# A recurrence, an MLP and a top-1 MoE on one core: other places for small products, routers, low parts, gathers and the end branch

## Chip, cores and metric

One core of one Trainium2 chip runs the whole kernel. The metric is the device time of one execution in microseconds. Engines are called as in the profile: PE (matmuls), PEld (weight loads), DVE, ACT, POOL, and SP, which issues most transfers.

## What is computed

Three stages follow one another; the output of each is the input of the next.

```
for t in range(768):                     # B=4, H=8, D=40
    y[:, :, t] = einsum('bhd,bhde->bhe', r_t, state)
    Sa = einsum('bhde,bhe->bhd', state, a_t)
    state = state * w_t[:, :, None, :] - einsum('bhd,bhe->bhde', Sa, b_t) + einsum('bhd,bhe->bhde', v_t, k_t)
x = y as [3072 tokens, 320]
x = relu(x @ w_in) ** 2 @ w_out          # 320 -> 2048 -> 320
e = argmax(x @ w_gate)                   # 8 experts, capacity 768 each
out = softmax(x @ w_gate)[e] * (relu(x @ w1[e]) @ w2[e])
```

## The kernel before

**Stages.** The sequence is cut into 12 segments of 64 tokens, and each segment into two chunks `c` of 32. The recurrence is solved chunk by chunk: per segment a lower-triangular system is inverted step by step on POOL (`rw.invert`, lines 333, with transposes to and from its layout on DVE at L220 and L242), and per chunk some hundreds of small products on PE (L336) carry the state. Their tiles are named `pr` (right side, `rw.right`), `psa` and `psd` (solve and turn), `ppq` (inner and mix), `pn` (state step, added into `zv` by DVE at L350), `py` (output, multiplied into `y` by DVE at L435 and L436) and `pa` (the next but one segment's matrix, `rw.lower`, read by `rw.put`, L201). `rw.scale` makes the scaled keys and decays of a segment by scans on DVE (L127, L140).

The MLP of a segment (256 columns for the 4 batch entries) is eight *bursts*: `up` makes two feature tiles `pl` of 16 matmuls (L494), in two pieces of 8, ACT forms the square `g` and its rounded copy `gh`, DVE the low part `gl` = g - gh (L705); `down` adds 12 matmuls into `acc` (L678) in two pieces, of which 4 read `gl`. A burst goes down after two later ones have gone up (`BEHIND = 2`). Before the segments there are 17 *routers* of two pieces each (`routers`): each folds one tile of `w_out` with `w_gate` (`ptg`, L501; `pog`, L678; `wogl`, L457), from `ao` tiles that DVE splits at L564 to L575.

The MoE handles 15 units of 256 tokens in its usual run, more behind a branch. Per unit: POOL gathers the unit's rows (`gather`, L1195, into the two buffers of `xg`), `turn` transposes them and makes the gate (L1216), four pairs of up (`upl`, L494) and down (`uacc`, L1187) follow, `end` multiplies by the gate (`uo`, DVE L1254 for the first 128 rows, ACT L1255 for the second), and two scatters on POOL write the result (L1265). Before the first unit the places of the first units are worked out by `early` (`ea_rank`, `solve_op` at L1009, `ea_inv`).

**What sets the order.** PE keeps program order for all these matmuls (`keep_in_program_order`); the other engines' orders come from a scheduler that follows priority, which is program order with offsets. The program is a loop over `s` and `c`; each chunk is a list of slots (`slot_a` to `slot_g`: output and right side; solve; burst; turn and inner; steps; mix; state step, and in chunk 1 the inverse, `lower` twice and `put`). After each slot `mlp(n)` issues `n` pieces of the MLP (or routers), where `n` comes from the tables `FIRST` (s = 0), `SECOND` (s = 1) and `SLOTS` (later):

```
for part, n in zip(parts, (FIRST, SECOND, SLOTS)[min(s, 2)][c]):
    with ahead(s):
        part()
    next(sc, None)
    mlp(n)
    ...
    next(side or iter(()), None)
```

`side` is the generator of `early`, which goes one step per slot. At the end `others` loads the number of units (L1307) and branches to further units; behind it L1598 loads `good`, a flag that the decays were in range, and L1599 branches to a slow path if not.

Of the kernel before, what the change touches and what calls it, by code (L numbers as in the profile page):

```python
# [11 lines left out]
F32 = mybir.dt.float32  # L12
# [504 lines left out]
class Mlp:  # L517
# [132 lines left out]
    def load_gate(self):  # L650
        self.turn = self.routed = self.done = 0
        self.wo = {}
        self.slow = self.behind = None
        self.pending = []
# [36 lines left out]
    def up(self, s, x, fp):  # L691
        nc, NT = self.nc, self.NT
        pl = self.psl.tile([128, 2, NT], F32, tag="pl", name=f"pl{s}_{fp}")
        for f in range(2):
            ft = fp * 2 + f
            product(self.tc, pl[:, f], self.wi, slice(ft * 128, (ft + 1) * 128), x, slice(0, NT))
            if f == 0:
                yield
        g = self.tile([128, 2, NT], f"g{s}_{fp}", "relu", 2)
        nc.scalar.activation(g, pl, AF.Relu)  # L700

        gh = self.tile([128, 2, NT], f"gh{s}_{fp}", "gh", 2, F32R)
        gl = self.tile([128, 2, NT], f"gl{s}_{fp}", "gl", 2, F32R)
        nc.scalar.activation(g, g, AF.Square)
        self.behind = (nc.scalar.copy(gh, g).ins, nc.vector.tensor_tensor(out=gl, in0=g, in1=gh.bitcast(F32), op=ALU.subtract).ins)  # L705
        self.pending.append([self.down, s, fp, gh, gl, None])
        yield

# [35 lines left out]
    def drain(self, n):  # L744

        while len(self.pending) > n:
            self.lows()
            f, *a = self.pending.pop(0)
            yield from f(*a)
# [92 lines left out]
class Moe:  # L842
# [6 lines left out]
    def __init__(self, keep, tc, ps, ml, ident, x1, logits, w1, w2, cap, cst, out):  # L849
        self.tc, self.nc, self.ps, self.ml, self.ident = tc, tc.nc, ps, ml, ident  # L850
        self.x1, self.logits, self.w1, self.w2, self.out = x1, logits, w1, w2, out
        nc = self.nc
        ct = keep.tile([128, cst.shape[1]], F32, tag="w_d", name="ct2")
        nc.scalar.dma_start(out=ct, in_=cst)
        self.c = {k: ct[:, v] for k, (n, v) in SETS.items() if n == 1}
        self.room = keep.tile([128, 2 * 16 * SC], F32, tag="kb_d", name="room")
        self.at, self.free = {}, 0
        self.new("ue", [128, NU * NEXP])
        cpi = self.new("cpi", [128, 1], I32)
        nc.scalar.dma_start(out=cpi, in_=cap.bitcast(I32)[0, 0:1].partition_broadcast(128))  # L860
# [5 lines left out]
        self.ui, self.idx, self.gate = {}, {}, {}  # L866
# [100 lines left out]
    def experts(self, end, name, j0, j1):  # L967
# [14 lines left out]
        self.total = ui[0:1, n:n + 1]  # L982

# [216 lines left out]

    def turn(self, j, xs):
# [35 lines left out]
    def down(self, j, w2, h, fp):  # L1237
        if fp == 0:
            self.acc = [self.ml.psa.tile([128, DX], F32, tag=f"acc{t}", name=f"uacc{j}_{t}")[:, 0:DM] for t in range(2)]
        for f in range(2):  # L1240
            ft = fp * 2 + f
            for t in range(2):
                cols = slice(t * 128, (t + 1) * 128)
                for n, (a, b) in enumerate(((h[0], w2[0]), (h[0], w2[1]), (h[1], w2[0]))):
                    self.mm(self.acc[t], lhsT=a[:, f, cols], rhs=b[:, ft],
                            start=ft == 0 and n == 0, stop=ft == FE // 128 - 1 and n == 2)
# [22 lines left out]
    def unit(self, j, units):  # L1269
# [7 lines left out]
        for fp in range(FE // 256):  # L1277
            if fp == 0 and more:
                nxt = self.gather(j + 1)
# [7 lines left out]
            if fp == TURN_AT and more:  # L1287
                self.ready[j + 1] = self.turn(j + 1, nxt)
# [16 lines left out]
    def others(self):  # L1305

        n = self.nc.values_load(self.total, min_val=0, max_val=NU)  # L1307
# [52 lines left out]
USUAL = 15  # L1360
BEHIND = 2
# [5 lines left out]
SLOTS = (2, 3, 2, 3, 2, 3, 3), (4, 3, 2, 2, 3)  # L1367
LEAD = 4
SECOND = (2, 2, 2, 1, 2, 1, 3), (3, 1, 2, 1, 2)
FIRST = (8, 4, 4, 4, 4, 2, 2), (2, 2, 2, 2, 0)  # L1370
# [14 lines left out]
def in_range(tc, pool, ps, consts, rng):  # L1385
# [5 lines left out]
    n = pool.tile([1, 1], I32, name="good")  # L1391
    p = ps.tile([128, 512], F32, tag="ps", name="pgood")
    tc.nc.tensor.matmul(p[0:1, 0:1], lhsT=f, rhs=consts["lane"], start=True, stop=True)
    V.tensor_copy(n, p[0:1, 0:1])
    return n
# [3 lines left out]
def tile_rwkv__mlp__moe(ctx, tc, wd, kb, ad, rv, wl, tok, vt, nat, w_in, w_out, w_gate, w1, w2, cap, cst1, cst2, cst3, out):  # L1399
# [9 lines left out]
    with ExitStack() as ph:  # L1409
# [56 lines left out]
        for s in range(NS):  # L1466
# [3 lines left out]
            for c in range(NC):  # L1470
# [7 lines left out]
                def slot_a():  # L1478
# [8 lines left out]
                    if last is not None:  # L1487
                        y = rw.out(*last)
                    rw.right(s, c)

                def slot_b():
# [18 lines left out]
                    if c == 1:  # L1510
                        next(st, None)
                        if s + 2 < NS:
                            rw.place(s + 2, 1)
                    elif s + 2 < NS:
# [36 lines left out]
                parts = slot_a, slot_b, slot_c, slot_d, slot_e, slot_f, slot_g  # L1551
                if c == 1:
                    parts = slot_a, slot_b, slot_d, slot_f, slot_g
# [21 lines left out]
        good = in_range(tc, cp, ps, consts, rng)  # L1575
# [112 lines left out]
```

## Time and profile before

| | us |
|---|---|
| three runs | 1059.51, 1054.82, 1055.98 |
| median | 1055.98 |
| profiled execution (the first of these) | 1059.51 |
| its span, first to last instruction | 1057.7 |
| PE, DVE, ACT, POOL busy | 883.6, 753.5, 617.0, 536.0 |
| mean granted clock of PE | 0.962 |

PE is busy for 84% of the span. The stages lie one after another in the trace: up to 172 us weights, routers and the first two chunks; from 172 to 694 us the recurrence with the MLP in its gaps, one segment per 53 us; to 785 us the last segment's MLP; to 1038 us the MoE; then the tail.

### The profile page before, as it was taken

How to read it: one execution, taken by the hardware profiler on the slowest of the kernel's cores; microseconds unless marked ns; L12 is line 12 of the kernel's file. 1: busy time of each engine (PE TensorE's matmuls, PEld its weight loads, DVE VectorE, ACT ScalarE, POOL GpSimd, SP SyncE). 2: the span in 40 equal slices, each digit the busy share in tenths (PEclk: the TensorE clock that was granted, in tenths of full speed). 3: DMA queues.
4: the chain of work that ended last, by engine and by line, in shares of the span. 5: the costliest groups of instructions: out<-in, count | busy, mean ns of one | idle time of the engine just before them, and what ended most of it. 6: DMA issues, size and time to landing. Idle time of an engine off the chain costs nothing.

```text
span 1057.7 us, 38842 instructions
## 1 busy us (share of the span) xinstructions
PE 883.6 (84%) x15962; PEld 833.8 (79%) x15962; DVE 753.5 (71%) x1691; ACT 617.0 (58%) x1618; POOL 536.0 (51%) x863
## 2 busy tenths in 40 slices
PE   1048555989898999899989989999899979999992
PEld 1047445888887998898888888999799979989992
DVE  7879778476768586768676766555579858778760
ACT  2135444765665666667656657765484757677650
POOL 4878508577686758686868685600000322223210
PEclk9999996999998999899999999999899999999996
DMA  7673464675565656565656564552682767777710
GB/s 210 194 235 94 142 177 115 222 207 168 143 189 139 180 151 180 148 180 165 175 145 180 148 169 135 150 154 67 223 267 80 237 177 222 226 203 228 212 54 9
DMA packets 91212, 177.17 MB, mean 168 GB/s; under 512 B 16489, under 2 KB 46827, under 8 KB 90060
## 3 DMA queue, kind: packets, MB, share of 16 engines
q1 hardware_dynamic: 87196, 164.99, 54.6%
q0 software_dynamic: 2880, 8.98, 2.5%
q8 instruction: 129, 2.11, 0.9%
q10 hardware_dynamic: 944, 0.57, 0.2%
q14 instruction: 63, 0.52, 0.2%
HBM read 138.52 MB, written 16.24 MB: 146 GB/s over the span
## 4 chain that ended last, share of the span: by engine, by line
PE 49%; DMA 15%; DVE 12%; ACT 9%; issue 7%; POOL 4%; SPq 2%; ACTq 0%; POOLq 0%; DVEq 0%
PE pl L494 12%; PE acc L678 11%; PE upl L494 7%; PE uacc L1187 7%; DMA out_dram<-uo,room 3%; DMA rq_a<-in_ad_dram 3%; PE pn L336 2%; POOL tl L333 2%; DVE zv L350 2%; DMA kb_d<-in_kb_dram 2%; PE ppq L336 2%; PE psa L336 2%; POOL tmp L333 2%; DVE rq_r L127 1%; DMA stage_lo<-in_w_out_dram 1%
## 5 line engine op out<-in xcount | busy, mean ns | idle before, releaser
L333 POOL TENSOR_TENSOR tl<-tl,tmp 128x126 f32<-128x126 f32 (+22 forms) x372 | 239.0, 642 | 29.0
L333 POOL TENSOR_TENSOR tmp<-solve_al,tl 128x126 f32<-128x126 f32 (+22 forms) x372 | 200.2, 538 | 61.2 <-DVE solve_al L220 28.6
L705 DVE TENSOR_TENSOR gl<-g,gh 128x512 fp32r<-128x512 f32 x96 | 66.7, 695 | 97.7 <-ACT gh L705 97.1
L678 PE MATMUL acc<-woh,gh 128*128 128x328 f32 x384 | 126.6, 335 | 4.0 <-ACT x L730 4.0
L678 PE MATMUL acc<-wol,gh 128*128 128x328 f32 x384 | 120.0, 318 | 0.8 <-issue 0.8
L494 PE MATMUL pl<-x_hi,wi_hi 128*128 128x256 f32 x384 | 118.2, 308 | 0.5 <-ACT x_hi L506 0.5
L494 PE MATMUL pl<-x_lo,wi_hi 128*128 128x256 f32 x384 | 112.4, 293 | 5.1 <-DVE x_lo L509 5.1
L494 PE MATMUL pl<-x_hi,wi_lo 128*128 128x256 f32 x384 | 112.1, 292 | 1.1 <-issue 1.1
L1265 POOL DMA_INDIRECT out_dram<-uo,room x30 | 34.3, 1142 | 152.4 <-DVE uo L1254 82.3
L1195 POOL DMA_INDIRECT xg<-x_dram,room x30 | 29.9, 997 | 145.4 <-DVE room L1027 69.6
L700 ACT ACTIVATE g<-pl 128x512 f32<-128x512 f32 x96 | 57.3, 597 | 68.4 <-PE pl L494 67.3
L678 PE MATMUL acc<-woh,gl 128*128 128x328 f32 x384 | 90.6, 318 | 0.0
L1187 PE MATMUL uacc<-w2h,hh 128*128 128x320 f32 x240 | 76.3, 318 | 11.9 <-DVE uo L1254 11.9
L494 PEld LDWEIGHTS pl<-x_lo,wi_hi 128*128 128x128 f32 x384 | 76.7, 200 | 5.4 <-DVE x_lo L509 5.4
L494 PEld LDWEIGHTS pl<-x_hi,wi_hi 128*128 128x128 f32 x384 | 76.4, 199 | 5.2 <-issue 1.2
L678 PEld LDWEIGHTS acc<-woh,gh 128*128 128x128 f32 x384 | 74.2, 193 | 7.2 <-ACT x L730 4.3
L494 PEld LDWEIGHTS pl<-x_hi,wi_lo 128*128 128x128 f32 x384 | 76.5, 199 | 0.0
L1187 PE MATMUL uacc<-w2h,hl 128*128 128x320 f32 x240 | 75.1, 313 | 0.0
L1187 PE MATMUL uacc<-w2l,hh 128*128 128x320 f32 x240 | 75.0, 312 | 0.0
L678 PEld LDWEIGHTS acc<-wol,gh 128*128 128x128 f32 x384 | 74.3, 194 | 0.0
L336 PE MATMUL pa<-kb_d,rq_a 40*32 40x64 f32 x1536 | 29.5, 236 | 52.8 <-DVE rq_a L167 47.2
L336 PEld LDWEIGHTS pa<-kb_d,rq_a 40*32 40x32 f32 x1536 | 26.5, 119 | 54.6 <-DVE rq_a L167 47.4
(264 smaller groups left out, 2710.3 us busy)
## 6 DMA issues: line engine op xcount, KB each, us to landing
wol<-wol SPq DMA_DIRECT2D x96, 328.0 KB
w<-in_w_dram SPq DMA_DIRECT2D x30, 640.0 KB
w<-in_w_dram SPq DMA_DIRECT2D x30, 512.0 KB
zv<-in_vt_dram SPq DMA_DIRECT2D x48, 208.0 KB
kb_d<-in_kb_dram SPq DMA_DIRECT2D x24, 320.0 KB
tk<-in_tok_dram SPq DMA_DIRECT2D x24, 320.0 KB
rx<-rt SPq DMA_DIRECT2D x192, 40.0 KB
zk<-tk SPq DMA_DIRECT2D x48, 160.0 KB
```

What stands on the lines that cost most here:

```text
L127: nc.vector.tensor_tensor_scan(out=rf[:, ::-1], data0=w[:rows, 1:][:, ::-1], data1=seed, initial=0.0, op0=ALU.mult, op1=ALU.add)
L333: self.last = f(*a, **k).ins
L336: self.tc.keep_in_program_order(self.nc.tensor.matmul(*a, **k))
L350: i = nc.vector.tensor_tensor(out=each(z[c ^ 1][rows, j, ps]), in0=each(z[c][rows, j, ps]), in1=pn[rows].rearrange("p (n y) e -> p n y e", ...
L494: tc.keep_in_program_order(tc.nc.tensor.matmul(out, lhsT=a, rhs=b, start=n == 0, stop=n == len(seq) - 1))
L678: self.tc.keep_in_program_order(self.nc.tensor.matmul(*a, **k))
L700: nc.scalar.activation(g, pl, AF.Relu)
L705: self.behind = (nc.scalar.copy(gh, g).ins, nc.vector.tensor_tensor(out=gl, in0=g, in1=gh.bitcast(F32), op=ALU.subtract).ins)
L1187: self.tc.keep_in_program_order(self.nc.tensor.matmul(*a, **k))
L1195: nc.gpsimd.indirect_dma_start(out=xg[:, 0:DX], out_offset=None, in_=self.x1, in_offset=bass.IndirectOffsetOnAxis(ap=self.idx[2 * j + t], ...
L1265: self.nc.gpsimd.indirect_dma_start(out=self.out, out_offset=bass.IndirectOffsetOnAxis(ap=self.to[:, n:n + 1], axis=0), in_=o[:, t], in_of ...
```

## The change

Seven edits, each small in code.

- **Slots.** `slot_r` takes `right` out of `slot_a`; chunk 1's `slot_g` is cut into `slot_g` (state step), `slot_h` (inverse, first `lower`, `put`) and `slot_i` (second `lower`, `put`). The tables have an entry for each; a chunk issues 18 and 14 pieces as before in `SLOTS`.
- **Routers.** `FIRST` gives 16 pieces (eight routers) after the first slot, none after the right side, and fewer between the solve and the mix.
- **Third scale.** `rw.scale(2)` is made in chunk 1 of segment 0 instead of chunk 0, and `place(2, 1)` in its last slot.
- **Low parts.** `gl` is issued after the first half of the next `up` (`low_parts`), no longer with `gh`.
- **Gathers.** `gather(j + 2)` is asked for right after `turn(j + 1)`, at the third of unit j's pairs, no longer at the start of unit j + 1; unit 1's with unit 0's turn.
- **Last pair of a unit.** The down products of the last pair go tile by tile: the six of the first accumulator, then the six of the second.
- **End branch.** `bad` (64 if out of range, else 0) is added to the number of units; one load serves both branches.

```diff
+                self.low_parts()
...
-        self.behind = (nc.scalar.copy(gh, g).ins, nc.vector.tensor_tensor(out=gl, in0=g, in1=gh.bitcast(F32), op=ALU.subtract).ins)
-        self.pending.append([self.down, s, fp, gh, gl, None])
+        self.behind = nc.scalar.copy(gh, g).ins, self.behind[1] if self.behind else None
+        self.pending.append([self.down, s, fp, gh, g, None])
+        self.whole.append(self.pending[-1])
...
+    def low_parts(self):
+        while self.whole:
+            p = self.whole.pop(0)
+            s, fp, gh, g = p[1:5]
+            p[4] = self.tile([128, 2, self.NT], f"gl{s}_{fp}", "gl", 2, F32R)
+            i = self.nc.vector.tensor_tensor(out=p[4], in0=g, in1=gh.bitcast(F32), op=ALU.subtract)
+            self.behind = self.behind[0], i.ins
...
+    def ask(self, j, units):
+        if j in units and j not in self.asked and 2 * j in self.idx:
+            self.asked[j] = self.gather(j)
...
+        order = [(f, t) for f in range(2) for t in range(2)]
+        if fp == FE // 256 - 1:
+            order = [(f, t) for t in range(2) for f in range(2)]
...
-                self.ready[j + 1] = self.turn(j + 1, nxt)
+                self.ready[j + 1] = self.turn(j + 1, self.asked.pop(j + 1))
+                self.ask(j + 2, units)
...
-SLOTS = (2, 3, 2, 3, 2, 3, 3), (4, 3, 2, 2, 3)
+SLOTS = (2, 2, 3, 2, 2, 2, 3, 2), (2, 2, 3, 2, 2, 1, 1, 1)
-SECOND = (2, 2, 2, 1, 2, 1, 3), (3, 1, 2, 1, 2)
-FIRST = (8, 4, 4, 4, 4, 2, 2), (2, 2, 2, 2, 0)
+SECOND = (0, 2, 2, 2, 1, 2, 1, 3), (1, 2, 1, 2, 1, 1, 1, 0)
+FIRST = (16, 0, 2, 2, 2, 2, 2, 2), (0, 2, 2, 2, 0, 0, 0, 0)
...
-                        if s + 2 < NS:
+                        if 0 < s < NS - 2:
                             rw.place(s + 2, 1)
-                    elif s + 2 < NS:
+                    if s + 2 < NS and c == (s == 0):
                         sc = rw.scale(s + 2)
...
-                    if c == 1 and more:
+                def slot_h():
+                    if more:
                         rw.inverted(s + 1)
                         if s + 2 < NS:
                             rw.lower(s + 2, 0)
                             rw.put()
-                            rw.lower(s + 2, 1)
-                            rw.put(True)
...
-        mo.others()
-    n = nc.values_load(good[0:1, 0:1], min_val=0, max_val=128)
-    with tc.If(n != 128):
+        n = nc.values_load(mo.state[0:1, 0:1], min_val=0, max_val=NU + BAD)
+        rest = ph.enter_context(tc.If(n > USUAL))
+        mo.others(n)
+        ph.close()
+    with tc.If(n >= BAD):
```

**Order on PE, steady segment, end of chunk 1** (state step `pn`, matrices `pa`, then the up products `pl` or down products `acc` of a burst; x32 means 32 rows alike). Before, both state steps and both matrices follow one another:

```order
L678 MATMUL acc_1_4429<-woh,gl_3_4533 128x328
L336 MATMUL pn_1_0_4818<-zv_117,zk_122 40x40 x16
L336 MATMUL pn_1_1_4837<-zv_117,zk_122 40x40 x16
L336 MATMUL pa_0_4862<-kb_d,rq_a_4163 32x64 x32
L336 MATMUL pa_1_4902<-kb_d,rq_a_4163 32x64 x32
L494 MATMUL pl_6_4938<-x_hi,wi_hi 128x256
```

Of the change:

```order
L336 MATMUL pn_1_0_4802<-zv_117,zk_122 40x40 x16
L336 MATMUL pn_1_1_4821<-zv_117,zk_122 40x40 x16
L678 MATMUL acc_0_4426<-woh,gh_3_4532 128x328
L678 MATMUL acc_0_4426<-wol_3_4535,gh_3_4532 128x328
L678 MATMUL acc_1_4427<-woh,gh_3_4532 128x328
L678 MATMUL acc_1_4427<-wol_3_4535,gh_3_4532 128x328
L678 MATMUL acc_0_4426<-woh,gl_3_4633 128x328
L678 MATMUL acc_1_4427<-woh,gl_3_4633 128x328
L336 MATMUL pa_0_4854<-kb_d,rq_a_4161 32x64 x32
```

Six down products now stand between the state step and the first matrix; six more follow it, and then the second matrix.

**Order on PE in the startup**, before (the first right side `pr` ahead of the routers, `psa` behind four of them):

```order
L336 MATMUL pa_1_833<-kb_d,rq_a_778 32x64 x32
L336 MATMUL pr_0_938<-zv_116,a_114 32x40 x32
L501 MATMUL ptg<-ct,ao_160 128x128 x2
L501 MATMUL ptg<-ct,ao_160 64x128
L501 MATMUL ptg<-ct,ao_171 128x128 x2
```

and of the change, the same place and the end of the routers:

```order
L501 MATMUL ptg<-ct,ao_389 128x128 x2
L501 MATMUL ptg<-ct,ao_389 64x128
L678 MATMUL pog<-wg,wt_1016 128x8 x3
L336 MATMUL pr_0_1039<-zv_116,a_114 32x40 x32
L336 MATMUL psa_0_1074<-rh_0_1072,tt_789 32x40 x32
L501 MATMUL ptg<-ct,ao_400 128x128 x2
L501 MATMUL ptg<-ct,ao_400 64x128
L678 MATMUL pog<-wg,wt_1030 128x8 x3
```

Before, four routers stand between this `pr` and `psa`, and four between `psa` and `psd`; of the change, eight stand ahead of `pr`, none between it and `psa`, and two between `psa` and `psd`.

**Order on DVE, steady segment, end of chunk 1** (`gl` the low part, `y` the output, `zv` the state, `x_lo` the next MLP input). Before:

```order
L705 TENSOR_TENSOR gl_6_4958<-g_6_4955,gh_6_4957 128x512
L435 TENSOR_TENSOR y_1_5012<-py_1_4979,qt_1_3887 128x320
L436 TENSOR_TENSOR y_1_5012<-py_1_4979,qt_1_3887 128x64
L393 TENSOR_TENSOR zv_116<-zv_116,g_4_3075 40x8x2x40 x2
L509 TENSOR_TENSOR x_lo<-pt,x_hi 128x8x32
```

Of the change:

```order
L435 TENSOR_TENSOR y_1_4987<-py_1_4954,qt_1_3862 128x320
L436 TENSOR_TENSOR y_1_4987<-py_1_4954,qt_1_3862 128x64
L393 TENSOR_TENSOR zv_116<-zv_116,g_4_3073 40x8x2x40 x2
L716 TENSOR_TENSOR gl_6_5209<-g_6_5000,gh_6_5002 128x512
L509 TENSOR_TENSOR x_lo<-pt,x_hi 128x8x32
```

The low part now stands behind the output and the state's decay.

On POOL the gathers and scatters of the MoE stand in the same order in both kernels.

## Rows read from the trace of the kernel before

**Rows 1.** Busy time by stage: us; each engine's busy us (instructions); granted clock; DMA share; GB/s.

```profile
0.00:172.00 172.00, 69.27 (x1391) 59.41 (x1391) 142.57 (x303) 63.34 (x184) 101.93 (x169) 0.95 0.60 173
222.50:648.70 426.20, 396.68 (x9322) 370.35 (x9321) 309.77 (x528) 269.07 (x632) 308.97 (x516) 0.96 0.59 163
785.00:1038.00 253.00, 240.82 (x1824) 237.86 (x1822) 190.69 (x583) 164.26 (x509) 58.00 (x54) 0.99 0.61 177
```

**Rows 2.** Waits of PE from 172 to 785 us: waiter, releaser; total us, times, longest.

```profile
PE pr L336 <- issue: 6.7, 4, 3.0
PE pt L501 <- DVE y L436: 6.3, 5, 3.2
PE pr L336 <- DVE zv L350: 6.1, 12, 1.7
PE pa L336 <- issue: 5.1, 6, 1.5
PE pz L307 <- issue: 1.8, 1, 1.8
PE ea_inv L1187 <- DVE solve_op L1009: 2.4, 1, 2.4
```

**Rows 3.** Timeline of PE round 587 us: start, us, instruction, idle before it in brackets.

```profile
583.90 1.88 PE L336 MATMUL pa<-kb_d,rq_a 40*32 40x64 f32 x120
587.31 0.32 PE L336 MATMUL pa<-kb_d,rq_a 40*32 40x64 f32 x8 [1.53 <-issue]
```

**Rows 4.** DMA queues from 585 to 587.3 us: packets, MB, share.

```profile
q8 instruction: 1, 0.02, 3.0%
```

**Rows 5.** Two stretches by busy time and granted clock (columns of rows 1).

```profile
587.30:590.70 3.40, 3.39 (x22) 3.30 (x22) 3.30 (x7) 1.79 (x4) 0.87 (x3) 0.54 0.71 200
437.00:444.20 7.20, 7.20 (x95) 6.86 (x96) 4.58 (x8) 5.80 (x15) 6.50 (x10) 0.53 0.31 87
```

**Rows 6.** Timeline of DVE: the same transpose in two successive segments.

```profile
427.77 1.23 DVE L242 STREAM_TRANSPOSE solve_tf<-tl 128x1024 f32<-128x1024 f32 x1
480.95 1.23 DVE L242 STREAM_TRANSPOSE solve_tf<-tl 128x1024 f32<-128x1024 f32 x1
```

**Rows 7.** Waits of POOL from 222 to 650 us.

```profile
POOL tl L333 <- DVE solve_tf L242: 57.3, 8, 9.0
POOL tmp L333 <- DVE solve_al L220: 21.6, 8, 2.9
```

**Rows 8.** Waits of DVE from 172 to 750 us.

```profile
DVE gl L705 <- ACT gh L705: 93.1, 45, 5.6
```

**Rows 9.** Timeline of DVE and PE: a low part and its first reader.

```profile
527.07 0.69 DVE L705 TENSOR_TENSOR gl<-g,gh 128x512 fp32r<-128x512 f32 x1 [1.29 <-ACT gh L705]
534.57 0.47 PE L678 MATMUL acc<-woh,gl 128*128 128x328 f32 x2
```

**Rows 10.** Timeline of PE (two rows) and DVE (three) in the startup.

```profile
77.37 1.29 PE L336 MATMUL psa<-rh,tt 32*32 32x40 f32 x64 [12.83 <-DVE tt L246]
165.02 0.87 PE L501 MATMUL pt<-ct,y 128*128 128x128 f32 x3 [10.05 <-DVE y L436]
72.31 1.25 DVE L242 STREAM_TRANSPOSE solve_tf<-tl 128x1024 f32<-128x1024 f32 x1 [4.50 <-POOL tl L333]
74.25 2.33 DVE L127 TENSOR_TENSOR_SCAN rq_r<-w_d,seed_q 104x1040 f32<-104x1040 f32 x1
118.87 0.29 DVE L565 TENSOR_SCALAR a<-a 128x256 f32<-128x256 f32 x1 [3.46 <-ACT a L564]
```

**Rows 11.** The placing of the first units, by busy time (columns of rows 1).

```profile
730.30:748.80 18.50, 16.07 (x287) 13.23 (x286) 17.41 (x74) 6.29 (x15) 0.00 (x0) 0.98 0.14 39
```

**Rows 12.** Waits of PE from 785 to 1045 us.

```profile
PE uacc L1187 <- DVE uo L1254: 11.9, 5, 5.3
```

**Rows 13.** Lines 1598 and 1308 on POOL's sequencer: count, ns min/median/max, first and last start.

```profile
L1598 POOLq TENSOR_LOAD <-good x1: 304/304/304, 1046.9 to 1046.9; - x1
L1308 POOLq INC_SWDGE_SEM  x1: 1379/1379/1379, 1045.5 to 1045.5; - x1
```

More of the change, by code (lines that the diff above doesn't have):

```diff
@@ L653, in load_gate @@
         self.slow = self.behind = None
-        self.pending = []
+        self.pending, self.whole = [], []
         for k in range(3):
@@ L702, in up @@
         gh = self.tile([128, 2, NT], f"gh{s}_{fp}", "gh", 2, F32R)
-        gl = self.tile([128, 2, NT], f"gl{s}_{fp}", "gl", 2, F32R)
         nc.scalar.activation(g, g, AF.Square)
-        self.behind = (nc.scalar.copy(gh, g).ins, nc.vector.tensor_tensor(out=gl, in0=g, in1=gh.bitcast(F32), op=ALU.subtract).ins)
-        self.pending.append([self.down, s, fp, gh, gl, None])
+        self.behind = nc.scalar.copy(gh, g).ins, self.behind[1] if self.behind else None
+        self.pending.append([self.down, s, fp, gh, g, None])
+        self.whole.append(self.pending[-1])
         yield
+    def low_parts(self):
[5 more added lines that the diff above has]
+            self.behind = self.behind[0], i.ins
     def down(self, s, fp, gh, gl, wol):
@@ L747, in drain @@
             self.lows()
+            if self.pending[0] in self.whole:
+                self.low_parts()
             f, *a = self.pending.pop(0)
@@ L865, in __init__ @@
         self.ready, self.w1s, self.w2s, self.to, self.done = {}, {}, {}, None, []
-        self.ui, self.idx, self.gate = {}, {}, {}
+        self.bad = None
+        self.ui, self.idx, self.gate, self.asked = {}, {}, {}, {}
     def space(self, ctx):
@@ L982, in experts @@
         self.total = ui[0:1, n:n + 1]
+        if self.bad is not None:
+            both = self.new(f"{name}_both", [128, 1])
+            V.tensor_tensor(out=both[0:1], in0=uf[0:1, n:n + 1], in1=self.bad[0:1], op=ALU.add)
+            self.state = self.new(f"{name}_state", [128, 1], I32)
+            V.tensor_copy(self.state[0:1], both[0:1])
     def places(self, slot, name):
@@ L1084, in first @@
                 self.ready[0] = self.turn(0, self.xs)
+                self.ask(1, range(USUAL))
     def late(self, first):
@@ L1239, in down @@
             self.acc = [self.ml.psa.tile([128, DX], F32, tag=f"acc{t}", name=f"uacc{j}_{t}")[:, 0:DM] for t in range(2)]
[L1240 to L1246, printed above, removed]
+        order = [(f, t) for f in range(2) for t in range(2)]
+        if fp == FE // 256 - 1:
+            order = [(f, t) for t in range(2) for f in range(2)]
+        for f, t in order:
+            ft, cols = fp * 2 + f, slice(t * 128, (t + 1) * 128)
+            for n, (a, b) in enumerate(((h[0], w2[0]), (h[0], w2[1]), (h[1], w2[0]))):
+                self.mm(self.acc[t], lhsT=a[:, f, cols], rhs=b[:, ft],
+                        start=ft == 0 and n == 0, stop=ft == FE // 128 - 1 and n == 2)
         if fp == FE // 256 - 1:
@@ L1277, in unit @@
         for fp in range(FE // 256):
-            if fp == 0 and more:
-                nxt = self.gather(j + 1)
+            if fp == 0:
+                self.ask(j + 1, units)
             h = self.up(j, x, w, fp)
@@ L1303, in run, with others @@
             pass
-    def others(self):
-        n = self.nc.values_load(self.total, min_val=0, max_val=NU)
+    def others(self, n=None):
+        if n is None:
+            n = self.nc.values_load(self.total, min_val=0, max_val=NU)
         with self.tc.If(n > USUAL):
@@ L1360 @@
 USUAL = 15
+BAD = 64
 BEHIND = 2
@@ L1390, in in_range @@
     V.tensor_scalar(out=f, in0=f, scalar1=0.0, scalar2=None, op0=ALU.is_equal)
-    n = pool.tile([1, 1], I32, name="good")
+    bad = pool.tile([128, 1], F32, name="bad")
     p = ps.tile([128, 512], F32, tag="ps", name="pgood")
     tc.nc.tensor.matmul(p[0:1, 0:1], lhsT=f, rhs=consts["lane"], start=True, stop=True)
-    V.tensor_copy(n, p[0:1, 0:1])
-    return n
+    V.tensor_scalar(out=bad[0:1], in0=p[0:1, 0:1], scalar1=128.0, scalar2=float(BAD), op0=ALU.is_lt, op1=ALU.mult)
+    return bad
 @with_exitstack
@@ L1488, in slot_a, with slot_r @@
                         y = rw.out(*last)
+                def slot_r():
                     rw.right(s, c)
@@ L1546, in slot_g, with slot_i @@
                             rw.put()
-                            rw.lower(s + 2, 1)
-                            rw.put(True)
+                def slot_i():
+                    if s == 0:
+                        rw.place(2, 1)
+                    if s + 2 < NS:
+                        rw.lower(s + 2, 1)
+                        rw.put(True)
                 rw.steady = s > 1
-                parts = slot_a, slot_b, slot_c, slot_d, slot_e, slot_f, slot_g
+                parts = slot_a, slot_r, slot_b, slot_c, slot_d, slot_e, slot_f, slot_g
                 if c == 1:
-                    parts = slot_a, slot_b, slot_d, slot_f, slot_g
+                    parts = slot_a, slot_r, slot_b, slot_d, slot_f, slot_g, slot_h, slot_i
                 for part, n in zip(parts, (FIRST, SECOND, SLOTS)[min(s, 2)][c]):
@@ L1574, in tile_rwkv__mlp__moe @@
         ml.add_y(xs[NS - 1], NC - 1, y)
-        good = in_range(tc, cp, ps, consts, rng)
+        mo.bad = in_range(tc, cp, ps, consts, rng)
         for _ in side:
```

## The prediction

> **What bounds the kernel now.** I read the busy time by stage first. PE is the bound from 222 us on: 396.7 of 426.2 us in the segments, 240.8 of 253.0 in the MoE; in the startup it is DVE, 142.6 of 172.0 us [rows 1]. So in the segments only what PE does not do, or does slowly, can be won: 29.5 us idle, and a granted clock of 0.96, which is (1 - 0.96) x 426 = 17 us of full speed missing.
>
> The waits of PE come second [rows 2]. Three rows say "issue", nothing the profile shows: 6.7 + 5.1 + 1.8 = 13.6 us in 11 waits. Two rows wait for DVE's `y` and `zv`: 6.3 + 6.1 = 12.4 us. The place of one issue wait is in the timeline: 120 products `pa` of 1.88 us together, then 1.53 us of nothing, then the last 8 [rows 3]; in the 2.3 us before its end one packet of 16 KB is moved by the queue named instruction [rows 4]. Every issue wait stands behind a run of over 100 such small products. I read this as PE outrunning the delivery of its own instructions: short ones are used up faster than they arrive.
>
> Third, the clock. After that wait, PE has 3.40 us at a granted 0.54; after the longest wait for `y`, 3.2 us, it has 7.20 us at 0.53 [rows 5, 2]. [...] The 17 us are mostly the echo of these waits.
>
> Fourth, what would bound next. A segment takes 480.95 - 427.77 = 53.2 us [rows 6]. POOL's inversion waits 57.3 / 8 = 7.2 us of that for the turned-in matrix, 21.6 / 8 = 2.7 for the second transpose [rows 7]. Its own work is 53.2 - 9.9 = 43.3 us; the second wait is the chain itself, and of the first some 2 us (the transpose, 1.23 us [rows 6], and the way there) cannot go. So a segment cannot fall under about 48 us by this change, which leaves POOL's work alone: at most 5.2 us each.
>
> **Shorter runs (slots and tables).** The same pieces are issued; nothing is added. At the end of chunk 1 the run of 64 `pn` and 128 `pa` becomes 64 each, with six to eight large products between; the right side is split from the output alike. The 13.6 us of issue waits should go almost whole; I take 12.5, bounded by 0 (they stay) and 13.6. Cover that could fail: segment 1 still has runs of 128.
>
> **Later low parts.** DVE stands still 93.1 us in 45 waits at the head of its queue, because `gl` waits for ACT's `gh` [rows 8], while `y` and `zv` are queued behind it. In the new order `y` and the state's decay stand ahead of `gl`. No work is added. Of the 12.4 us of waits for `y` and `zv` I take 10 away, as the slots also put products of the MLP between each small product and its reader; bounds 0 and 12.4. What is late next is `gl`: one low part ended at 527.76 and was first read at 534.57, 6.8 us later [rows 9]. Half an up and a few DVE instructions fit in that, so I cost it at nothing; without that cover each burst would wait, which is the slower case below.
>
> **Clock.** If most waits of over a microsecond go, of the 17 us I take 10; bounds 0 and 17.
>
> **Sum in the segments:** 12.5 + 10 + 10 = 32.5 us, under the ceiling of 8 x 5.2 = 42. The three overlap, and a PE that comes sooner meets DVE, ACT and the inversion earlier: I take four fifths, **-26 us**, 50 us a segment. Bounds: 0 and -42.
>
> [...]
>
> **Startup (routers first, scale later).** `psa` waits 12.83 us for `tt` in the trace, and a scan of 2.33 us of the third scale stands on DVE between the transpose and `tt`; DVE itself had waited 4.50 us for POOL, and at 118.87 us it waited 3.46 us for ACT's copy of a raw weight tile [rows 10], whose buffers a POOL instruction held that now stands earlier. The change lets four more routers run in the 12.83 us, and `psa` come 2.3 us sooner. But the end of this stage is DVE's: PE waits 10.05 us for `y` at 165.02 us [rows 10] with DVE at work, and DVE's work up to there is the same. Only its idle time can go: of the 3.46 and 4.50 us I take half, **-4 us**. Bounds: +2 (eight routers hold up the first right side) and -10.
>
> **Placing the first units.** `early` goes a slot sooner, so `ea_rank` leads the last `py`. From the ranks to the last `solve_op` DVE is busy for 17.41 of 18.50 us and PE for 16.07 [rows 11]; `ea_inv` waits 2.4 us [rows 2]. Of PE's work there some 5 us now lie on the wrong side, so the wait grows: **+2.5 us**; bounds 0 and +4.
>
> **MoE.** On POOL the order of gathers and scatters is unchanged, so the gathers asked for sooner are not issued sooner: 0. The last pair's order ends the first accumulator six products sooner; at 240.82 us / 1824 = 0.13 us [rows 1] that is 0.8 us for DVE's `uo`, the first scatter and the gather behind it. Five waits of PE for `uo`, 11.9 us together [rows 12], shrink by up to 0.8 each: **-3 us**; bounds 0 and -4.
>
> **Tail.** A load of 0.30 us [rows 13] goes, with the gap round it; the 1.38 us on POOL at the end of the branch [rows 13] stays. With the `uo` of the last unit 0.8 us sooner: **-1 us**; bounds 0 and -1.5. The flag costs two tiny DVE instructions, hidden by the work of 753 us there: 0.
>
> **Sum:** -26 - 4 + 2.5 - 3 - 1 = **-31.5 us**. The profiled execution took 1059.5 us, so 1028.0; the median of the runs, 1056.0, stands 3.5 us below it, and gives **1024.5 us**.
>
> **Rivals.**
>
> [...]
>
> *The inversion takes the place of the waits.* The slots put `inverted` and the transposes into a slot of their own, behind down products, and DVE may reach them later. With 51 us a segment instead of 50, (53.2 - 51) x 8 = 17.6, sum -23, **1033 us**. For it: POOL needs 48 of 50 us; against: it still waited 7.2 us a segment.
>
> *The gathers are not sooner*: this part does not do what it says, by the order on POOL. It is in the sum at nothing.
>
> *Slower: low parts that come too late.* `gl` stands behind scans of 2.33 us and the like; if its start moves by more than 6.8 us, `down` waits on PE. A wait of 1 us and the clock's 1.6 us behind it [rows 5] are 2.6 us a burst. From one burst in eight (12 of 96, 31 us) the gain is gone; with one in four, 24 x 2.6 = 62 us, **1087 us**. For it: DVE is busy for 310 of 426 us and its order is by priority. Against: DVE loses the 93 us at the head of its queue.
>
> **How the numbers follow.** Forecast 0.62; issue waits stay 0.15; inversion 0.11; slower 0.06; gains and losses that cancel 0.06. The range goes down to where the bounds of the small terms meet a loop gain of 32.5 (-32.5 - 10 + 0 - 4 - 1.5 = -48: 1008) and up past the first rival, with the small terms at their bad ends (-12 + 2 + 4 - 2 = -8: 1048; I stop at 1047). A measurement of this kernel can tell about 0.5%, 5 us, from no change. Faster 0.88, within 0.06, slower 0.06.
>
> **What would show it.** Right: almost no issue waits and a granted clock of 0.98 or more in the segments; 50 us between two transposes; POOL's wait for the turned-in matrix near 4 us; `gl` no longer at the head of DVE's waits; the `pt` of 165.02 us near 161; `ea_inv` waiting 4 to 5 us; waits for `uo` of 8 to 9 us. Wrong: issue waits as before behind shorter runs; PE waits of `acc` for DVE's `gl`; a segment still over 52 us; that `pt` later than 165 us.

## The result, and the profile after

The changed kernel takes **1025.72 us** (median of 4 runs, 1023.86 to 1026.23); the kernel before, 1055.4 us (4 runs). The ratio is 0.969, with a 95% interval of 0.966 to 0.973: faster, 1.2 us above the forecast. The profiled execution took 1025.28 us, its span 1023.4. Here and below, executions that took over 1.5% longer than the fastest of the same kernel are left out of the times.

Busy time and granted clock by stage, of the changed kernel; the columns and the stages are those of [rows 1]:

```profile
0.00:167.00 167.00, 71.04 (x1392) 60.56 (x1392) 142.61 (x304) 62.54 (x184) 103.54 (x169) 0.95 0.62 178
217.50:619.20 401.70, 389.23 (x9315) 358.29 (x9315) 311.75 (x530) 270.09 (x632) 314.13 (x526) 1.00 0.62 173
757.00:1004.00 247.00, 242.07 (x1827) 239.39 (x1825) 188.72 (x582) 163.19 (x504) 59.64 (x55) 0.99 0.60 180
```

Where the time went, by first instructions that both traces have (the second `x_lo`; `psa` of segment 2's and of segment 10's first chunk; the last `psa`; the product `ea_turned`; the first `upl`; the last `uacc`; the end of the span; each figure is rounded by itself):

| stage | before | after | difference | forecast |
|---|---|---|---|---|
| startup, to the second `x_lo` | 171.6 | 166.5 | -5.1 | -4 |
| first segments | 51.4 | 52.0 | +0.6 | |
| eight segments in the steady order | 426.2 | 400.7 | -25.5 | -26 for all segments |
| last segments | 72.1 | 70.7 | -1.4 | |
| placing the first units | 28.2 | 28.6 | +0.4 | +2.5 |
| last MLP | 35.1 | 38.6 | +3.5 | 0 |
| MoE | 252.8 | 246.4 | -6.4 | -3 |
| tail | 20.2 | 20.0 | -0.2 | -1 |
| sum (of the span) | 1057.7 | 1023.4 | -34.3 | -31.5 |

The segments give the bulk: of the same products, PE is busy 389.2 us instead of 396.7, and its idle time falls from 29.5 to 12.5 us. The shorter busy time goes with the granted clock, 1.00 there and 0.96 before [rows 1].

Waits of PE from 167 to 757 us, of the changed kernel (waiter, releaser; total us, times, longest), which answer to [rows 2]:

```profile
PE ea_inv L1206 <- DVE rq_ov L1022: 3.6, 1, 3.6
PE pz L307 <- issue: 2.6, 1, 2.6
PE pr L336 <- issue: 2.5, 4, 0.9
PE acc L678 <- DMA wol<-wol: 2.0, 1, 2.0
PE pr L336 <- DVE zv L350: 1.6, 6, 0.4
...
PE pa L336 <- issue: 0.5, 1, 0.5
```

The three issue rows fall from 13.6 to 5.6 us; the waits for `y` are gone, those for `zv` 1.6 us.

POOL's waits from 210 to 640 us [rows 7] and the turned-in matrix on DVE in two successive segments [rows 6], of the changed kernel:

```profile
POOL tmp L333 <- DVE solve_al L220: 37.7, 9, 6.6
POOL tl L333 <- DVE solve_tf L242: 17.3, 8, 6.0
```

```profile
410.43 1.25 DVE L242 STREAM_TRANSPOSE solve_tf<-tl 128x1024 f32<-128x1024 f32 x1 [0.74 <-POOL tl L333]
459.06 1.25 DVE L242 STREAM_TRANSPOSE solve_tf<-tl 128x1024 f32<-128x1024 f32 x1 [0.18 <-POOL tl L333]
```

This segment took 48.6 us, near the 48 us worked out before, and DVE now waits for POOL at both its ends. The eight segments average 50.1 us. The inversion is still not what PE waits for: no wait of PE for it stands in these segments, and PE's own 389.2 us are 48.7 us a segment.

### The profile page after: what moved, and what is told of

Read it like the earlier page. It is cut to its first block, busy times and chain, and to the rows that moved or that the text cites. A ratio compares the mean times of both kernels' runs of the same rounds, so it can differ in the third digit from the quotient of the medians.

```text
span 1023.4 us, 38810 instructions
## 1 busy us (share of the span) xinstructions
PE 881.0 (86%) x15962; PEld 826.7 (81%) x15962; DVE 752.9 (74%) x1693; ACT 619.1 (60%) x1618; POOL 538.8 (53%) x863
## 4 chain that ended last, share of the span: by engine, by line
PE 38%; DMA 16%; DVE 15%; POOL 13%; issue 11%; ACT 5%; SPq 1%; POOLq 0%; DVEq 0%; ACTq 0%
PE pl L494 10%; PE acc L678 9%; POOL tl L333 6%; POOL tmp L333 5%; DMA out_dram<-uo,room 5%; PE upl L494 4%; PE uacc L1206 4%; DVE rq_r L127 3%; PE pn L336 2%; DMA lr<-in_rv_dram 2%; DMA rq_a<-in_ad_dram 2%; DMA a<-rq_a 2%; DMA wol<-wol 2%; DMA xg<-x_dram,room 1%; PE pa L336 1%
## 5 line engine op out<-in xcount | busy, mean ns | idle before, releaser
L333 POOL TENSOR_TENSOR tl<-tl,tmp 128x126 f32<-128x126 f32 (+22 forms) x372 | 236.0, 634 | 29.0
L333 POOL TENSOR_TENSOR tmp<-solve_al,tl 128x126 f32<-128x126 f32 (+22 forms) x372 | 207.0, 556 | 75.4 <-DVE solve_al L220 47.4
L1214 POOL DMA_INDIRECT xg<-x_dram,room x30 | 32.1, 1071 | 157.8 <-DVE x_lo L509 69.9
L494 PE MATMUL pl<-x_lo,wi_hi 128*128 128x256 f32 x384 | 110.0, 286 | 5.1 <-DVE x_lo L509 5.1
L494 PE MATMUL pl<-x_hi,wi_lo 128*128 128x256 f32 x384 | 109.8, 286 | 0.0
L494 PEld LDWEIGHTS pl<-x_lo,wi_hi 128*128 128x128 f32 x384 | 74.1, 193 | 5.5 <-DVE x_lo L509 5.4
L494 PEld LDWEIGHTS pl<-x_hi,wi_hi 128*128 128x128 f32 x384 | 73.8, 192 | 5.5 <-ACT g L701 1.1
L494 PEld LDWEIGHTS pl<-x_hi,wi_lo 128*128 128x128 f32 x384 | 74.0, 193 | 0.0
```

Of the source, the lines that this page charges most:

```text
L333: self.last = f(*a, **k).ins
L494: tc.keep_in_program_order(tc.nc.tensor.matmul(out, lhsT=a, rhs=b, start=n == 0, stop=n == len(seq) - 1))
L1214: nc.gpsimd.indirect_dma_start(out=xg[:, 0:DX], out_offset=None, in_=self.x1, in_offset=bass.IndirectOffsetOnAxis(ap=self.idx[2 * j + t], ...
```

## Experiments

Parts of the change were made alone, or undone alone. Each run has a kernel before on the same chip beside it: 1060.0 us (13 runs) for experiments 1, 2, 6 and 7, 1056.6 for 4, 5, 8 and 9, 1056.8 for 3, 10, 11 and 12 (7 runs each). Single runs of one kernel on these chips spread over 5 to 15 us, so the parts are read from the stages and the waits of the traces, and from times only where these are far apart.

**1. The slots alone**, on the kernel before (in segments 0 and 1 its tables are mapped so that no piece moves):

```diff
-SLOTS = (2, 3, 2, 3, 2, 3, 3), (4, 3, 2, 2, 3)
+SLOTS = (2, 2, 3, 2, 2, 2, 3, 2), (2, 2, 3, 2, 2, 1, 1, 1)
+                def slot_r():
                     rw.right(s, c)
...
+                def slot_h():
+                    if more:
                         rw.inverted(s + 1)
...
+                def slot_i():
+                    if s + 2 < NS:
+                        rw.lower(s + 2, 1)
+                        rw.put(True)
```

> The kernel before with the slots alone (right side and the end of chunk 1 split, tables of segments 2 and later; startup, low parts, MoE and tail as before). Theory (PE outran its instructions, and small products stood directly behind their producers): issue waits fall from 13.6 us to under 6, the waits for zv and y partly; a segment takes about 51 us instead of 53.2; 1056 - 17 = 1039 us (1032 to 1045). Rival one (issue waits have another cause): waits stay, under 6 us gained, 1050 or more. Rival two (the low parts are the whole gain): 1050 or more, with DVE's wait for gh at 93 us as before.

Measured: 1024.6 and 1037.8 us (two runs), the span of the second 1036.0. The eight segments take 401.5 us instead of 426.2: all of the segments' gain, and 50.2 us a segment where 51 were expected. The segments by busy time, then waits of PE, then the first wait of DVE, all from 221.8 to 623.3 us:

```profile
221.80:623.30 401.50, 389.96 (x9313) 359.59 (x9312) 310.18 (x528) 269.08 (x629) 312.15 (x519) 0.99 0.62 173
```

```profile
PE pz L307 <- issue: 3.5, 1, 3.5
PE pr L336 <- DVE zv L350: 2.0, 6, 0.6
```

```profile
DVE gl L705 <- ACT gh L705: 5.9, 7, 1.8
```

The last row is the surprise. Over the same segments, 222.9 to 649.1 us, the kernel before has

```profile
DVE gl L705 <- ACT gh L705: 53.7, 32, 3.7
```

In the program `gl` still follows `gh` at once, but the order on DVE is the scheduler's, and with the slots it is another one. At the end of a segment, before (three rows of DVE, then PE's next product) and here (DVE):

```profile
435.71 0.69 DVE L705 TENSOR_TENSOR gl<-g,gh 128x512 fp32r<-128x512 f32 x1 [2.40 <-ACT gh L705]
436.32 0.48 DVE L435 TENSOR_TENSOR y<-py,qt 128x320 f32<-128x320 f32 x1
436.72 0.21 DVE L436 TENSOR_TENSOR y<-py,qt 128x64 f32<-128x64 f32 x1
436.95 0.52 PE L501 MATMUL pt<-ct,y 128*128 128x128 f32 x3 [3.17 <-DVE y L436]
```

```profile
420.47 0.49 DVE L435 TENSOR_TENSOR y<-py,qt 128x320 f32<-128x320 f32 x1
420.88 0.21 DVE L436 TENSOR_TENSOR y<-py,qt 128x64 f32<-128x64 f32 x1
...
422.86 0.69 DVE L705 TENSOR_TENSOR gl<-g,gh 128x512 fp32r<-128x512 f32 x1 [0.91 <-ACT gh L705]
```

A low part stands right ahead of `y` at the ends of six of segments 1 to 10 before, and of one here (segment 1, whose table is the old one). All three waits of PE for `y` of over 0.3 us before follow a low part that had waited 1.8 to 2.4 us for `gh`; here PE has no wait for `y`. The longer waits for `zv` (0.6 us and more) have another head of the queue: each follows `rq_a`, which had waited 2.4 to 3.0 us for a DMA. The longest of them before (DVE, then PE), and DVE's waits for that DMA in the eight segments, before and here:

```profile
241.96 1.48 DVE L167 TENSOR_TENSOR rq_a<-rq_a,w_d 104x1024 f32<-104x1024 f32 x1 [2.67 <-DMA rq_a<-in_ad_dram]
245.02 0.26 PE L336 MATMUL pr<-zv,a 104*32 104x40 f32 x2 [1.75 <-DVE zv L350]
```

```profile
DVE rq_a L167 <- DMA rq_a<-in_ad_dram: 22.3, 8, 4.4
```

```profile
DVE rq_a L167 <- DMA rq_a<-in_ad_dram: 5.8, 7, 1.3
```

**2. The later low parts alone**, on the kernel before:

```diff
             if f == 0:
                 yield
+                self.low_parts()
...
-        self.behind = (nc.scalar.copy(gh, g).ins, nc.vector.tensor_tensor(out=gl, in0=g, in1=gh.bitcast(F32), op=ALU.subtract).ins)
-        self.pending.append([self.down, s, fp, gh, gl, None])
+        self.behind = nc.scalar.copy(gh, g).ins, self.behind[1] if self.behind else None
+        self.pending.append([self.down, s, fp, gh, g, None])
+        self.whole.append(self.pending[-1])
```

> The kernel before with the later low parts alone. Theory: DVE's wait for gh falls from 93 us to under 45, PE's waits for y and zv by 6 to 10 us, the issue waits stay near 13.6 us; 1056 - 10 = 1046 us (1040 to 1051). Rival (the head of DVE's queue held nobody up on PE): same as before, 1053 to 1058. Slower rival (low parts too late): PE waits for gl, over 1060.

Measured: 1055.6 us (9 runs, 1051.3 to 1059.0), ratio 0.996 (0.993 to 0.999). The eight segments take 424.2 us, 2.0 less than before. Waits of DVE and of PE from 221.2 to 645.4 us:

```profile
DVE gl L716 <- ACT gh L705: 54.6, 33, 3.7
```

```profile
PE pr L336 <- DVE zv L350: 6.1, 15, 0.9
PE pa L336 <- issue: 5.2, 6, 1.3
PE pt L501 <- DVE y L436: 4.5, 4, 2.2
PE pr L336 <- issue: 3.3, 3, 2.3
```

Waits and segments are those of before; the expectation of 10 us missed. The rival's time came, but not its reason: the edit left DVE's order as it was, with a low part right ahead of `y` at the same six segment ends, and PE still waits behind it.

```profile
431.37 0.69 DVE L716 TENSOR_TENSOR gl<-g,gh 128x512 fp32r<-128x512 f32 x1 [2.41 <-ACT gh L705]
431.98 0.48 DVE L435 TENSOR_TENSOR y<-py,qt 128x320 f32<-128x320 f32 x1
432.61 0.52 PE L501 MATMUL pt<-ct,y 128*128 128x128 f32 x3 [2.21 <-DVE y L436]
```

**3. The low parts of before in the changed kernel** (the opposite of experiment 2: the lines of `up` as before, the rest changed).

> The changed kernel with the low parts directly behind their rounded copies, as before. Theory (from the run with the low parts alone, which moved little): the later low parts bring nothing, 1024 to 1028 us, DVE's wait for gh under 50 us also without them. Rival (they bring the waits for y and zv down once the slots are split): 1031 to 1036 us, waits for y and zv of 6 to 10 us.

Measured: 1027.3 us (4 runs, 1024.9 to 1029.7); the changed kernel, run again beside it, 1024.2 (1017.8 to 1027.4). In the eight segments, 403.7 us, DVE waits 6.8 us for `gh`, PE 1.9 us for `zv` and not for `y`; eight kernels with the segments of the change take 400.5 to 405.9 us there. No low part stands right ahead of `y` here either. So the rival, that the low parts pay once the slots are split, falls.

**4. Low parts at the last place**: issued only when their down product is about to be.

```diff
             if f == 0:
                 yield
-                self.low_parts()
```

> The changed kernel with each low part issued only when its down product is about to be issued, not after the first half of the next up. Theory (some 7 us of slack cover the present place, nothing covers this one): PE waits for gl in most bursts, over half a microsecond each, and the clock falls behind the longer ones; 1025.7 + 50 = 1075 us (1045 to 1110). Rival (program order matters little, since the scheduler places DVE's work by its own estimate): within 5 us of the changed kernel.

Measured: 1026.6 us (1021.6 to 1029.9). The expectation missed by 48 us, and its rival held: PE has no wait for `gl`. DVE's order shows why: the scheduler puts the low part much where it stands of the change, behind `y` and the state (at three of ten segment ends between the state's two halves).

```order
L435 TENSOR_TENSOR y_1_4987<-py_1_4954,qt_1_3860 128x320
L436 TENSOR_TENSOR y_1_4987<-py_1_4954,qt_1_3860 128x64
L393 TENSOR_TENSOR zv_116<-zv_116,g_4_3071 40x8x2x40 x2
L715 TENSOR_TENSOR gl_6_5224<-g_6_4998,gh_6_5000 128x512
```

So this run didn't try a low part that comes too late; what that would cost stays open.

**5. The instruction stream moved by 128 instructions**, on the kernel before: 64 products (64 weight loads, 64 matmuls) are made twice in the startup, where PE is idle.

```diff
                     rw.right(s, c)
+                    if s == 0 and c == 0:
+                        rw.right(s, c)
```

> The kernel before with the 64 products of the first right side issued twice in the startup, where PE is idle: 128 instructions more on PE, half of a 16 KB block. Theory (PE waits for the next block of its instructions, and waits where a block ends inside a run of small products): the time stays within 5 us of before, but the issue waits stand at other places in the segments; the one of 1.53 us before the last 8 products pa moves or goes, and each wait still ends some 2.3 us after the start of a 16 KB packet. Rival (some property of the long run itself, such as a full queue or the clock): the waits stand at the same products of the same segments.

Measured: 1053.4 us, one run. An issue wait in its segments, in the timeline of PE (start, us, instruction, idle before it):

```profile
376.06 0.77 PE L336 MATMUL pr<-zv,a 104*32 104x40 f32 x62
379.87 0.23 PE L336 MATMUL pr<-zv,a 128*32 128x40 f32 x2 [3.04 <-issue]
```

Nothing waits at this product in the kernel before, and the wait of [rows 3] has gone. Counting PE's products from the start of the program (a product is a weight load and a matmul), the products behind issue waits of over 0.8 us, from 172 us on, are number

```
before:   2371 2498 3514 3641 4657 4912 5800 9484 9992 10500 11643
steps:      127 1016  127 1016  255  888 3684  508   508  1143    (127 x 1 8 1 8 2 7 29 4 4 9, within one)
shifted:  2372 2627 6056 7072 8215 11899
steps:      255 3429 1016 1143 3684                                (127 x 2 27 8 9 29, within one)
```

All steps are multiples of 127 products, 254 instructions, within one. Divided by 127, all numbers of both lists leave 85 to 88, though in the second every product of the segments has a number higher by 64. So the places follow the count, not the product, and the rival, some property of the run itself, falls. Each of these 17 waits ends 2.3 to 3.0 us after the start of a 16 KB packet of the queue named instruction, as expected; that queue moves 129 such packets in the kernel before, where PE and PEld have 31924 instructions, 247 for each packet. So PE waits at the end of a block of some 254 of its own instructions (the 128 of this edit are half of one), mostly where that end falls into a run of small products (three of the 17 stand ahead of a large one). An estimate from [rows 3] gives a reason for small ones: 127 products `pa` at 1.88 / 120 us each last 2.0 us, less than the 2.3 us.

**6. The startup of before in the changed kernel.**

```diff
-FIRST = (16, 0, 2, 2, 2, 2, 2, 2), (0, 2, 2, 2, 0, 0, 0, 0)
+FIRST = (0, 8, 4, 4, 4, 4, 2, 2), (0, 2, 2, 2, 2, 0, 0, 0)
...
-                    if s + 2 < NS and c == (s == 0):
+                    elif s + 2 < NS:
                         sc = rw.scale(s + 2)
```

> The changed kernel with the startup of before (routers 8, 4, 4, 4, ... and the third scale in chunk 0). Theory: the startup is bound by DVE and the change took 4 to 5 us of its idle time, so 1025.7 + 5 = 1031 us, and the first up product of the MLP stands at 165 to 167 us instead of 161. Rival: what is lost at the start is taken up later by slack in the segments, 1026 to 1027.

Measured: 1032.1 us (1025.4 to 1038.9). The second `x_lo` stands at 170.4 us instead of 166.5, 3.9 later: in the five kernels with the startup of before it stands at 169.3 to 171.6 us, in the nine with the new one at 166.0 to 167.5. The eight segments take 401.9 us, 1.2 more than in the changed kernel, so they take nothing up. The span of this trace is 1023.6 us, as long as the changed kernel's, as its MoE is 2.8 us shorter; why, no run shows.

**7. The last pair of a unit in the old order**, in the changed kernel.

```diff
-        if fp == FE // 256 - 1:
-            order = [(f, t) for t in range(2) for f in range(2)]
```

> The changed kernel with the down products of a unit's last pair in the old order. Theory one (order of the products makes uo 0.8 us sooner at five waits): PE's waits for uo come back to 5 to 10 us, +4 us, 1030. Theory two (the MoE's 6.4 us come from elsewhere, such as the gathers): 1025 to 1027, no waits for uo.

Measured: 1028.1 us (3 runs, 1022.0 to 1036.3), too wide to tell. The trace is of a longer execution (1040.7 us), so its MoE is read beside those of the others. It takes 254.0 us instead of 246.4, and PE's waits for `uo` are back (763 to 1018 us; 0.2 us in the changed kernel):

```profile
PE uacc L1206 <- DVE uo L1277: 9.2, 5, 3.2
```

All kernels of this study stand so: five with the old order have a MoE of 250.7 to 256.9 us, all seven others that share the gate's place 243.6 to 248.0.

**8. The gathers asked for as before**, in the changed kernel.

```diff
-                self.ask(j + 2, units)
```

(and the same for unit 1 in `first`.)

> The changed kernel with each gather asked for at the start of the unit before, as in the kernel before. Theory (POOL's order is the same, so nothing moves): 1025 to 1027 us, gathers issued at the same distance from the scatters. Rival (the earlier place moves ACT's copy of the gathered rows, or frees a buffer, and is part of the MoE's 6.4 us): 1028 to 1032.

Measured: 1027.0 us (1022.6 to 1028.4); its MoE takes 246.5 us, the changed kernel's 246.4. The gathers asked for sooner do nothing.

**9. Placing the first units a step per slot of before**, in the changed kernel.

```diff
-                    next(side or iter(()), None)
+                    if part not in ((slot_r,) if c == 0 else (slot_r, slot_h, slot_i)):
+                        next(side or iter(()), None)
```

> The changed kernel in which the placing of the first units goes one step per slot only at the slots that the kernel before had. Theory: the wait before ea_inv falls from 3.6 to about 2.4 us and the ranks no longer lead the last output; 1025.7 - 2 = 1024 us. Rival: the work is only moved behind the last output, and the last MLP stage, whose transfers take 0.97 of the DMA engines, ends at the same time: 1025 to 1027.

Measured: 1023.3 us (1017.5 to 1026.9). The placing takes 25.9 us instead of 28.6 and the last MLP 36.9 instead of 38.6, together 4.4 less; the wait before `ea_inv` is 2.1 us. In the six kernels with the step of before the two stages take 61.0 to 64.2 us together, in the eight with the new one 65.1 to 67.4. So the change's loss of 3.9 us there is the earlier step. The times don't tell it from the changed kernel.

**10 and 11. The gate behind `uo`.** `uo` stands on DVE behind the gate of the next unit, and that waits for its gather. The timeline of the kernel before near its longest wait for `uo`, DVE and then POOL:

```profile
859.44 0.16 DVE L1216 TENSOR_REDUCE gate<-xg 128x1 f32<-128x8 f32 x1 [5.88 <-DMA xg<-x_dram,room]
860.86 0.16 DVE L1216 TENSOR_REDUCE gate<-xg 128x1 f32<-128x8 f32 x1 [0.86 <-DMA xg<-x_dram,room]
863.43 0.54 DVE L1254 TENSOR_SCALAR uo<-uacc,gate 128x320 f32<-128x320 f32 x1
```

```profile
848.89 0.98 POOL L1265 DMA_INDIRECT out_dram<-uo,room  x1 [3.83 <-DVE hl L1233]
854.07 0.98 POOL L1265 DMA_INDIRECT out_dram<-uo,room  x1 [4.20 <-ACT w2h L1143]
855.36 0.99 POOL L1195 DMA_INDIRECT xg<-x_dram,room  x1 [0.30 <-PE upl L494]
...
864.25 1.28 POOL L1265 DMA_INDIRECT out_dram<-uo,room  x1 [6.62 <-DVE uo L1254]
```

These steps can be read as a ring: `uo`, its scatter, some 5 us later the second scatter, the next gather, 4 us later the gate, and 2.57 us after that the next `uo`. Two experiments keep the gate's readers and `uo` in program order on DVE, which puts the gate behind `uo`, the second with the step of experiment 9 as well.

```diff
-            V.tensor_reduce(out=most, in_=xg[:, 0:NEXP], axis=AX.X, op=ALU.max)
+            self.tc.keep_in_program_order(V.tensor_reduce(out=most, in_=xg[:, 0:NEXP], axis=AX.X, op=ALU.max))
```

> The changed kernel with the readers of the gathered rows that make the gate kept in program order with uo on DVE, so that uo no longer stands behind a gather that has not landed. Theory (the MoE is held by a ring: uo, scatter, next scatter, gather, gate, uo): PE's wait of 2.9 us near the fourth unit and the half clock behind it go, the MoE stage falls from 246.4 to about 241 us; 1025.7 - 5 = 1021 us. Rival (the gathered rows are late for the transposes on PE as well, so the wait only changes its name): 1024 to 1027, with PE waiting for x or for pt.

> The last one together with the placing of the first units one step per slot of the kernel before. Theory: the two gains add, 1025.7 - 5 - 2 = 1019 us, both stages as in the single runs. Rival: as the single gate run, within 2 us.

Measured: 1025.2 us (1020.9 to 1030.8) and 1020.1 us (3 runs, 1015.3 to 1028.9), beside 1024.2 for the changed kernel again. The MoE takes 249.5 and 244.2 us, where 241 were expected and the changed kernel's two traces have 246.4 and 244.5. For the first, the rival held; the second is too wide to tell by its times, and its gain in the trace is that of experiment 9 (placing and last MLP 63.0 us). Waits of POOL and PE in the MoE of the first (765 to 1010 us):

```profile
POOL xg L1214 <- ACT gate L1242: 115.7, 14, 26.2
```

```profile
PE pt L501 <- DMA xg<-x_dram,room: 6.6, 2, 3.3
```

The gate now lets go of the gathered rows later, the next gather waits for that buffer, and PE waits for the rows instead. No version clearly beats the changed kernel.

**12. The changed kernel again.**

> The changed kernel again, unaltered, as the measure of the other three on the same chip: 1023 to 1028 us.

Measured: 1024.2 us (1017.8 to 1027.4), the eight segments 400.5 us, the MoE 244.5.

## Why the prediction was right

The sum was 2.8 us off by the trace, and the range and the sign held. That it came so close is in part luck: terms were off by up to 4.5 us, some too large and some too small, and single runs of one kernel differ by more. In the upper end of the range a term of -2 stands without a bound behind it; without it that end is 1050. The 12 us that this end takes off, what the loop gains if the issue waits stay, no run shows: their three rows fell from 13.6 to 5.6 us.

**Issue waits: the mechanism right, the size off.** The forecast took 12.5 of 13.6 us away; the same three rows keep 5.6, so 8.0 went. "Every issue wait stands behind a run of over 100 such small products" was misread: the 1.8 us of `pz` [rows 2] stand behind a run of 67, and the same place keeps a wait of the change (before, then after):

```profile
329.14 1.12 PE L336 MATMUL psa<-rh,tt 32*32 32x40 f32 x64
330.19 0.53 PE L307 MATMUL pz<-ct,zv 40*104 40x40 f32 x3
332.51 0.48 PE L307 MATMUL pz<-ct,zv 40*104 40x40 f32 x5 [1.79 <-issue]
```

```profile
319.21 0.35 PE L307 MATMUL pz<-ct,zv 40*104 40x40 f32 x6
322.11 0.24 PE L307 MATMUL pz<-ct,zv 40*104 40x40 f32 x2 [2.55 <-issue]
```

So runs cut to 64 were not short enough. Experiment 5 shows the cause: PE waits where a block of some 254 of its instructions ends inside a run of small products, 1.53 us [rows 3] and 3.04 us (experiment 5), and the wait ends 2.3 to 3.0 us after the start of a 16 KB packet.

**Waits for `y` and `zv`: the size right, the edit wrong, the cause right for `y` alone.** The 12.4 us did go to 1.6. For `y` the rows bear the forecast out: PE waits where a low part that waits for `gh` stands ahead of `y` on DVE, and not where `y` stands ahead (experiments 1 and 2). But this new order is not the work of the later low parts: they leave DVE's order and 10.6 us of the waits as they were, while the slots alone bring the order and leave 2.0 us. For `zv` the step that failed is "`gl` waits for ACT's `gh` [rows 8], while `y` and `zv` are queued behind it": its longer waits stand behind `rq_a` and its DMA. No run changes DVE's order and nothing else, so what the new places of the products on PE add is open, and so is why the scheduler orders DVE otherwise with them. The fall of DVE's wait for `gh` from 53.7 to 5.9 us is no measure of the gain: all of DVE's idle time in the eight segments falls by 25 us, what the stretch got shorter by, and other waits grow, that of `x_lo` for ACT from 11.1 to 26.7 us.

**Clock.** 10 us were taken; PE's busy time for the same products fell by 7.5 us, at a granted clock of 1.00 instead of 0.96. Together 8.0 + 10.8 + 7.5 = 26.3 of the 32.5 us, and the stretch gained 24.5 by busy and idle time. The four fifths for overlap made up for sizes that were too large. In the eight segments of the kernel before, the granted clock is 0.50 in seven stretches of 3.4 or 6.8 us, 30.7 us together; half of that, 15.4 us, is nearly all of the 17. A stretch of 3.41 us loses 1.7 us so, near the 1.6 of the slower rival (3.40 us at 0.54 [rows 5]). Nine of PE's 13 waits of 1.0 us or more there stand up to 5.4 us ahead of these stretches or in them; four, of 1.0 to 1.2 us, have none behind them. Of the change there is one such stretch, 3.4 us behind the wait of 2.55 us. Outside the eight segments and the MoE a lower clock did not show in the time: over the whole span it is 0.911 in the trace of experiment 5 and 0.962 in that of the kernel before, in the eight segments 0.96 in both and in the MoE 1.00 and 0.99, and experiment 5 took 1053.4 us, the kernel before 1059.5.

**Startup.** -4 forecast, -5.1 in the trace, 3.9 by experiment 6. "`psa` come 2.3 us sooner" failed: it starts at 81.44 us instead of 77.37, behind the eight routers and the first right side, without the wait for `tt`. That did not reach the stage's end. PE still waits 10.6 us for `y` there, as DVE's work, 142.6 us in both, is the same.

**Placing.** The mechanism was right, the place of the loss only partly: the placing itself lost 0.4 us and the last MLP, costed at nothing, 3.5. Together 3.9 for a forecast of 2.5; the earlier step of `early` is the cause (experiment 9).

**MoE: mis-sized, -6.4 instead of -3.** "Six products sooner" was miscounted: the first accumulator ended nine products into the twelve and now ends six into them, so it is three sooner, 0.4 us. Nor does `uo` follow the accumulator where PE waits: from the third to the twelfth unit it starts 2.50 to 2.57 us behind the second reader of the gate, 2.17 to 2.23 us of the change, and 2.51 to 2.57 us with the old order again (experiment 7). In the change one weight piece no longer stands ahead of it on DVE. The waits that the profile puts down to DVE's `uo` fell from 11.9 to 0.2 us, where 8 to 9 were forecast; one of 2.9 us, put down to ACT, ends right behind a `uo` too (834.46 to 835.00, PE goes on at 835.15), with a granted clock of 0.50 from 834.5 to 841.3 us. Between the third and the twelfth `uo` a unit took 16.8 us before (842.30 to 993.55) and takes 16.1 now (815.43 to 960.00), which is PE's own work, 240.82 / 15 = 16.1 us [rows 1]. How 0.3 us at each `uo` takes so much of the waits is open: that they add up round the ring was not shown. That the gathers asked for sooner bring nothing was right (experiment 8).

**Tail.** The load of 0.30 us went, but the stage only lost 0.2 us, not 1.

**Rivals.** The inversion did not take the place of the waits: POOL's wait for the first transpose fell to 17.3 / 8 = 2.2 us (4 were forecast), and its wait for the second rose from 21.6 us in 8 waits to 37.7 us in 9. The part of the first that cannot go is less than the 2 us taken: POOL starts 0.06 to 0.12 us behind the end of the transpose in both traces, and its shortest waits in the change are 1.34 us. The slower rival's late low part never came about, and experiment 4 failed to make one, as DVE's order did not follow the program there.

## What to carry over

Where a scheduler sets an engine's order, the edit that moves an instruction in the program need not be the one that moves it on the engine; read the order of every trial from its trace before an edit is credited or cleared. Runs of many short products on PE had a cost of their own here at the ends of instruction blocks; with long products between them the three rows of issue waits fell from 13.6 to 5.6 us. Before a wait is costed, find the instruction that the late one really follows: `uo` followed the gate, not the accumulator.

## What was not expected of the hardware

PE's issue waits of over 0.8 us, from 172 us on, stand multiples of a fixed step apart, 127 products of a weight load and a matmul each, within one, and moving the stream by 64 products moves every one of them (experiment 5). Behind 64 `psa` and 6 `pz` there is still such a wait, 2.6 us, in the changed kernel.
